# When a kernel asks for its values and its raw weights: two load rules of an attention, MLP and MoE kernel

## The chip, the cores and the metric

The kernel runs on one core of one Trainium2 chip. The metric is the device time of one execution in microseconds (us). Engines are named as in the profile: PE is TensorE (PEld its weight loads), DVE is VectorE, ACT is ScalarE, POOL is GpSimd, SP is the queue that starts the DMA transfers.

## The reference, cut

Three stages follow each other; 2304 tokens of width 512 run through all of them.

```python
# 1: attention, 4 batches x 8 heads x 576 positions x 64
q_d, k_d, v_d = means over 4 neighbouring positions
out_up = repeat(softmax(scale * q_d @ k_d.T) @ v_d, 4)
out_local = softmax(where(abs(i - j) < 4, scale * q @ k.T, -1e9)) @ v
x = out_up + out_local                      # 2304 x 512
# 2: MLP, w_in 512 x 2048, w_out 2048 x 512, both handed over as float64
x = softplus(x @ w_in) @ w_out
# 3: top-1 MoE over 8 experts (512 x 1024 x 512), gated by softmax of the router
```

## The kernel before

**Attention** is cut into jobs, listed in `jobs`. For each batch and pair of heads there is a `Down` job (the attention over means) and three `Local` jobs (one per 192 positions). A job has six stages (`st_T`, `st_S`, `st_E`, `st_N`, `st_Ta`, `st_PV`), and `attn_to` runs them software-pipelined, each stage some jobs behind the one before.

**Loads.** `loads` holds pairs (job number, function), sorted; after the first stage of job n, `load_after(n)` issues all loads whose number has come. A `Down` job's q, k and v (tiles `qr`, `kr`, `vr`, L136 and L139) are asked for four jobs ahead. A pair of `Local` jobs shares one value tile `lv` (L286, three DMAs of 70 KB with 256-byte rows); it is asked for right after the first `Local` job of the pair has been appended, with number `len(jobs) - 1`, that is, that job itself. The pool has three `lv` buffers.

**The MLP** works in six blocks of 384 tokens, each in 16 chunks: `mlp_H` (PE, tile `ph`, L571 in block 0, L574 later), a softplus on ACT and DVE (`gN`, L589 in block 0), `mlp_Y` (PE, tile `py`, L611 in block 0, L614 later). Block 0 multiplies in float32; later blocks split each weight chunk into two float32r parts: `split` copies on ACT (L474) and subtracts on POOL (L475) into tags `wis` and `wos`, two slots each.

**Float64 weights.** The 32 weight chunks (16 of w_in, 16 of w_out) arrive as int32 pairs and are turned into float32 by `from_f64`: one ACT operation (L435, |high word|) and four DVE operations (L436 to L439) per chunk of 128x512, into `wi` or `wo`. `conv` is the list of chunks; `conv_to` converts up to a count and calls `load_raw(i + 2)` before and after each. The raw tile of 512 KB (L452 for w_in, L456 for w_out) takes one of the six slots of the tag `raw`, which it shares with `vr`, with `qr` and `kr` of batches 1 to 3, and later with the outputs. `qr` and `kr` of batch 0 use the slots of `wis` and `wos`, which no split needs yet.

**What sets the order.** The program is recorded in the order of the loops; a scheduler then places instructions on each engine by priority and by when a slot is free. Each engine runs its own list strictly in order. SP too: a DMA that waits for a slot holds up all that are listed behind it. The last stretch before block 1 starts at about 180 us; block 0 with the conversion lies at about 64 to 180 us, the first attention jobs ahead of it. `warm` adds a small matmul (L265) behind attention matmuls in jobs 4 to 11.

Of the kernel before, what the change touches and what calls it, by code (L numbers as in the profile page):

```python
# [11 lines left out]
I32 = mybir.dt.int32  # L12
# [6 lines left out]
B, H, S, D = 4, 8, 576, 64  # L19
# [5 lines left out]
NPAIR = H // 2  # L25
# [5 lines left out]
NTH = S // TH  # L31
# [12 lines left out]
RAWB = 6  # L44
RAWB = 6
# [8 lines left out]
def band_attention__softplus_mlp__top1_moe(  # L54
# [44 lines left out]
    mlp = ctx.enter_context(tc.tile_pool(name="mlp", bufs=2))  # L99
# [4 lines left out]
    def ahead(n):  # L104

        return tc.high_priority(n) if n else nullcontext()
# [260 lines left out]
    jobs = []  # L367
    loads = []
    for b in range(B):
        if b in []:  # L370
            order = [(j, hp) for hp in range(NPAIR) for j in range(2)] + [(2, hp) for hp in range(NPAIR)]
        else:
            order = [(j, hp) for j in range(NTH) for hp in range(NPAIR)]
        for j, hp in order:
            if j == 0:
                jobs.append(Down(b, hp))
                loads.append((len(jobs) - 4, jobs[-1].load))
            jobs.append(Local(b, j, hp))
            if hp % 2 == 0:
                loads.append((len(jobs) - 1, jobs[-1].load_v))  # L380
    NJ = len(jobs)
    loads.sort(key=lambda x: x[0])

# [45 lines left out]
    def from_f64(raw, dst, on_g):  # L429

        lo, hi = raw[:, :, 0], raw[:, :, 1]
        t = mlp.tile([128, 512], I32, tag="cva", name="cva", bufs=2)
        A.activation(t.bitcast(F32), hi.bitcast(F32), AF.Abs)  # L435
        (G if on_g else V).tensor_scalar(t.bitcast(F32), t.bitcast(F32), F64_LEAST, None, ALU.max)  # L436
        V.tensor_scalar(t, t, 3, 0x3FFFFFF8, ALU.logical_shift_left, ALU.bitwise_and)
        V.scalar_tensor_tensor(t, hi, -0x40000000, t, ALU.bitwise_and, ALU.bitwise_or)
        V.scalar_tensor_tensor(dst.bitcast(I32), lo, 29, t, ALU.logical_shift_right, ALU.bitwise_or)  # L439
# [7 lines left out]
    def load_raw(n):  # L447
        while lpos[0] < min(n, len(conv)):
            kind, c = conv[lpos[0]]
            raw = mlp.tile([128, 512, 2], I32, tag="raw", name="raw", bufs=RAWB)  # L450
            if kind == "i":
                nc.sync.dma_start(  # L452
                    out=raw.rearrange("p (c f) w -> p c (f w)", c=CC),
                    in_=w_in[:, c * 128:(c + 1) * 128].bitcast(I32).rearrange("(c p) f -> p c f", p=128))
            else:
                nc.sync.dma_start(out=raw.rearrange("p f w -> p (f w)"),  # L456
                                  in_=w_out[c * 128:(c + 1) * 128, :].bitcast(I32))
            raws[lpos[0]] = raw
            lpos[0] += 1

    def conv_to(n):
        while cpos[0] < min(n, len(conv)):
            i = cpos[0]
            load_raw(i + 2)
            kind, c = conv[i]
            with ahead(0 if started[0] else -50):
                from_f64(raws.pop(i), wi[:, c].rearrange("p c f -> p (c f)") if kind == "i" else wo[:, c, :], i < 0)
            cpos[0] += 1
            load_raw(i + 2)

    def split(src, tag):
        w = mlp.tile([128, 2] + list(src.shape)[1:], F32R, tag=tag, name=tag, bufs=2)
# [5 lines left out]
    wis, wos = {}, {}  # L478
# [212 lines left out]
    for st in range(12 + LAG):  # L691
        attn_to(pre_end[st])
        if st >= C0 - 5 + LAG:
            conv_to((st - C0 + 5 - LAG) * CR // 4 + 1)
        if st == 9 + LAG:
            split_wi(0, 0)
# [15 lines left out]
    for i, (n, c) in enumerate(seq):  # L712
# [14 lines left out]
        if n == 0:  # L727
            conv_to(max(cpos[0], 3 + 2 * c + 1, CB + (33 - CB) * (2 * c + 1) // 26))
# [9 lines left out]
        if n == 0:  # L738
            conv_to(max(cpos[0], 3 + 2 * c + 2, CB + (33 - CB) * (2 * c + 2) // 26))
# [61 lines left out]
```

## Time and profile before

| | |
|---|---|
| three runs | 806.86, 814.97, 822.22 us; median 814.97 |
| profiled execution | 816.7 us, of which the span from first to last instruction is 814.8 |
| PE busy | 788.8 us (97% of the span), PEld 690.1 |
| DVE, ACT, POOL busy | 469.0, 452.8, 449.6 us (58, 56, 55%) |
| mean granted clock | 0.979 of full speed |
| HBM traffic | 45.05 MB read, 9.44 MB written, mean 67 GB/s |

PE's ends are modelled, so its busy share says where it did not wait, not that it ran at its peak. In the page's 40 slices (20 us each) PE's busy tenths begin 5899899 and stay at 9 afterwards; its granted clock reads 5 in the third slice. DVE's tenths are 6 to 9 in the first eight slices, and DMA's 9936677 in the first seven, after which both fall.

### The profile page before, as it was taken

The page shows a single profiled execution, that of the slowest core. Times are in us where ns is not written, and L with a number is a line of the kernel's source. Part 1 is how long each engine was busy: PE and PEld are TensorE (multiplying, and loading weights), DVE is VectorE, ACT ScalarE, POOL GpSimd, SP SyncE. Part 2 cuts the span into 40 slices and gives each one's busy share as a digit, 9 for nine tenths or more (in the row PEclk, how much of TensorE's full clock was granted, in tenths as well). Part 3 has the DMA queues.
Part 4 walks back from the last instruction along what each step waited for, and adds up shares of the span by engine and source line. Part 5 has one row for each costly group of instructions (what it writes and reads, how often), then busy time and mean ns, then how long its engine had stood idle before and what let it go on. Part 6 is the DMA issues. An engine that isn't in the chain of part 4 may idle for free.

```text
span 814.8 us, 14060 instructions
## 1 busy us (share of the span) xinstructions
PE 788.8 (97%) x5101; PEld 690.1 (85%) x5102; DVE 469.0 (58%) x1008; ACT 452.8 (56%) x1153; POOL 449.6 (55%) x435
## 2 busy tenths in 40 slices
PE   5899899999999999999999999999999999999996
PEld 4785556568899989989999999999998899898985
DVE  6958899736866667688655665648552422212111
ACT  5836676446556565766565656565654444444342
POOL 3534321315745566666656666666665666666662
PEclk9959999999989999999999999999999999999999
DMA  9936677302200321021000100063010201011011
GB/s 173 208 82 171 202 237 213 89 22 79 60 11 19 85 48 39 26 56 61 2 11 10 34 21 1 1 245 117 1 39 39 79 4 75 1 39 39 1 39 43
DMA packets 82167, 55.47 MB, mean 68 GB/s; under 512 B 61081, under 2 KB 73899, under 8 KB 82091
## 3 DMA queue, kind: packets, MB, share of 16 engines
q1 hardware_dynamic: 82091, 54.50, 23.9%
q8 instruction: 42, 0.69, 0.3%
q14 instruction: 34, 0.28, 0.1%
HBM read 45.05 MB, written 9.44 MB: 67 GB/s over the span
## 4 chain that ended last, share of the span: by engine, by line
PE 85%; DVE 6%; ACT 3%; DMA 2%; SPq 1%; issue 1%; POOL 0%; DVEq 0%; POOLq 0%; ACTq 0%
PE ph L574 32%; PE py L614 19%; PE py L658 12%; PE ph L571 4%; PE py L611 4%; PE pO L340 3%; PE pS L306 3%; PE pA L331 2%; PE pO L249 1%; PE pT L169 1%; PE pS L210 1%; PE pA L239 1%; DVE g L596 1%; SPq L136 1%; DMA qr<-in_q_dram 1%
## 5 line engine op out<-in xcount | busy, mean ns | idle before, releaser
L614 PE MATMUL py<-g,wos 128*128 128x384 f32 x960 | 192.4, 344 | 0.0
L574 PE MATMUL ph<-xT,wis 128*128 128x384 f32 x960 | 184.3, 339 | 0.3 <-ACT qkT L175 0.2
L614 PEld LDWEIGHTS py<-g,wos 128*128 128x128 f32 x960 | 166.9, 190 | 4.9 <-issue 1.7
L574 PEld LDWEIGHTS ph<-xT,wis 128*128 128x128 f32 x960 | 166.8, 188 | 2.5 <-issue 0.8
L475 POOL TENSOR_TENSOR wis<-wi,wis 128x512 fp32r<-128x512 f32 x80 | 107.0, 1338 | 60.6 <-ACT wis L474 55.0
L475 POOL TENSOR_TENSOR wos<-wo,wos 128x512 fp32r<-128x512 f32 x80 | 107.7, 1347 | 41.4 <-ACT wos L474 41.3
L574 PE MATMUL ph<-yT,wis 128*128 128x384 f32 x576 | 108.2, 336 | 0.0
L658 PE MATMUL py<-wos,g 128*128 128x512 f32 x432 | 106.6, 392 | 0.0
L574 PEld LDWEIGHTS ph<-yT,wis 128*128 128x128 f32 x576 | 101.5, 188 | 3.5
L601 DVE SCALAR_TENSOR_TENSOR g<-ph,g 128x384 fp32r<-128x384 f32 x48 | 26.7, 557 | 131.2 <-ACT g L600 131.2
L580 ACT ACTIVATE ga<-ph 128x384 f32<-128x384 f32 x96 | 46.8, 487 | 93.7 <-PE ph L574 76.3
L658 PEld LDWEIGHTS py<-wos,g 128*128 128x128 f32 x432 | 80.3, 188 | 15.3 <-ACT wis L474 0.6
L475 POOL TENSOR_TENSOR wos<-w2s,wos 128x512 fp32r<-128x512 f32 x48 | 64.0, 1334 | 48.7 <-ACT wos L474 48.7
L475 POOL TENSOR_TENSOR wis<-w1s,wis 128x512 fp32r<-128x512 f32 x48 | 61.8, 1288 | 30.5 <-ACT wis L474 30.4
L320 ACT ACTIVATE ls<-ls,lst 128x70 f32<-128x70 f32 x144 | 49.3, 344 | 42.0 <-DVE lst L314 38.1
L595 DVE SCALAR_TENSOR_TENSOR ga<-ph,ga 128x384 f32<-128x384 f32 x80 | 44.1, 551 | 49.6 <-ACT ga L582 49.1
L474 ACT CAST wos<-wo 128x512 fp32r<-128x512 f32 x80 | 49.5, 619 | 36.3 <-PE py L614 36.0
L597 DVE TENSOR_TENSOR g<-ga,g 128x384 fp32r<-128x384 f32 x80 | 65.7, 821 | 2.0
L326 POOL TENSOR_TENSOR ls<-ls,lst 128x210 f32<-128x210 f32 x48 | 29.1, 608 | 57.7 <-DVE lst L325 42.6
L600 ACT ACTIVATE g<-ph 128x384 fp32r<-128x384 f32 x48 | 23.6, 492 | 57.1 <-PE py L658 31.7
L596 DVE CAST g<-ga 128x384 fp32r<-128x384 f32 x80 | 49.9, 623 | 3.6 <-PE py L614 0.5
L582 ACT ACTIVATE ga<-ga 128x384 f32<-128x384 f32 x96 | 50.4, 525 | 1.9
(130 smaller groups left out, 1173.0 us busy)
## 6 DMA issues: line engine op xcount, KB each, us to landing
raw<-in_moe_w_in_dram SPq DMA_DIRECT2D x16, 512.0 KB
raw<-in_moe_w_out_dram SPq DMA_DIRECT2D x16, 512.0 KB
lv<-in_v_dram SPq DMA_DIRECT2D x72, 70.0 KB
qr<-in_q_dram SPq DMA_DIRECT2D x32, 144.0 KB
kr<-in_k_dram SPq DMA_DIRECT2D x32, 144.0 KB
vr<-in_v_dram SPq DMA_DIRECT2D x16, 288.0 KB
ydram<-y SPq DMA_DIRECT2D x12, 384.0 KB
yb<-ydram SPq DMA_DIRECT2D x6, 768.0 KB
```

Of the source, the lines that this page charges most:

```text
L320: A.activation(s[:, i, :], s[:, i, :], AF.Exp, bias=st[:, 0, i], accum_out=st[:, 1, i])
L474: A.copy(w[:, 0], src)
L475: G.tensor_tensor(out=w[:, 1], in0=src, in1=w[:, 0].bitcast(F32), op=ALU.subtract)
L571: T.matmul(ps[:, :TB], wi[:, c, cc, :], xT[n][:, cc, :], start=(cc == 0), stop=(cc == CC - 1))
L574: T.matmul(ps[:, :TB], wt[:, w, cc, :], xT[n][:, x, cc, :], start=(i == 0), stop=(i == 3 * CC - 1))
L580: A.activation(a, ps[:, :TB], AF.Abs)
L582: A.activation(a, a, AF.Ln, bias=1.0)
L595: V.scalar_tensor_tensor(a, ps[:, :TB], 0.0, a, ALU.max, ALU.add)
L596: (A.copy if n < 1 else V.tensor_copy)(g[:, 0, :], a)
L597: (G if n < 1 else V).tensor_tensor(out=g[:, 1, :], in0=a, in1=g[:, 0, :].bitcast(F32), op=ALU.subtract)
L614: T.matmul(yps[n][dc][:, :TB], w[:, a, dsl], g[:, b, :], start=(c == 0 and i == 0), stop=(c == NC1 - 1 and i == 2))
L658: T.matmul(yps[n][t], g[:, a, ts], w[:, b, :], start=(c == 0 and i == 0), stop=(c == NC2 - 1 and i == 2))
```

## The change

The first edit adds three to the job number at which a `Local` pair's value tile is asked for, with an upper limit near the end of the list. The second puts the raw float64 chunks of w_in into the two slots of `wis` and those of w_out into the two slots of `wos`, and leaves the `raw` slots to the attention tiles and outputs. The third asks for raw chunks three ahead of the conversion instead of two.

```diff
             if hp % 2 == 0:
-                loads.append((len(jobs) - 1, jobs[-1].load_v))
+                loads.append((min(len(jobs) + 2, B * NPAIR * (NTH + 1) - 1), jobs[-1].load_v))
 ...
-            raw = mlp.tile([128, 512, 2], I32, tag="raw", name="raw", bufs=RAWB)
+            raw = mlp.tile([128, 512, 2], I32, tag={"i": "wis", "o": "wos"}[kind], name="raw", bufs=2)
 ...
             i = cpos[0]
-            load_raw(i + 2)
+            load_raw(i + 3)
 ...
             cpos[0] += 1
-            load_raw(i + 2)
+            load_raw(i + 3)
```

SP's list of DMAs, from the second `Down` job's loads at the start of the program, before (x2 and x3 are so many DMAs):

```order
L136 DMA kr<-in_k_dram 96x6x64 x2
L139 DMA vr<-in_v_dram 72x4x256
L286 DMA lv<-in_v_dram 70x4x64 x3
L136 DMA qr<-in_q_dram 96x6x64 x2
L136 DMA kr<-in_k_dram 96x6x64 x2
L139 DMA vr<-in_v_dram 72x4x256
L136 DMA qr<-in_q_dram 96x6x64 x2
L136 DMA kr<-in_k_dram 96x6x64 x2
L139 DMA vr<-in_v_dram 72x4x256
L286 DMA lv<-in_v_dram 70x4x64 x3
L452 DMA raw<-in_moe_w_in_dram 128x4x256 x2
```

The same place of SP's list, of the change:

```order
L136 DMA kr<-in_k_dram 96x6x64 x2
L139 DMA vr<-in_v_dram 72x4x256
L136 DMA qr<-in_q_dram 96x6x64 x2
L136 DMA kr<-in_k_dram 96x6x64 x2
L139 DMA vr<-in_v_dram 72x4x256
L136 DMA qr<-in_q_dram 96x6x64 x2
L139 DMA vr<-in_v_dram 72x4x256
L136 DMA kr<-in_k_dram 96x6x64 x2
L286 DMA lv<-in_v_dram 70x4x64 x3
L452 DMA raw<-in_moe_w_in_dram 128x4x256
L456 DMA raw<-in_moe_w_out_dram 128x1024
```

The first value tile has moved from behind the second `Down` job to behind the fourth, and the first chunks follow it at once.

POOL's list at the end of batch 0's `Down` jobs (at about 34 to 52 us in the trace), before:

```order
L326 TENSOR_TENSOR ls<-ls,lst 128x210 x2
L475 TENSOR_TENSOR wis<-wi,wis 128x512
L150 TENSOR_TENSOR vr<-vr 72x4x128
L475 TENSOR_TENSOR wis<-wi,wis 128x512
L153 TENSOR_TENSOR vs<-vr 72x2x64 x2
L326 TENSOR_TENSOR ls<-ls,lst 128x210 x2
L475 TENSOR_TENSOR wos<-wo,wos 128x512
L150 TENSOR_TENSOR vr<-vr 72x4x128
```

The same place of POOL's list, of the change:

```order
L326 TENSOR_TENSOR ls<-ls,lst 128x210 x2
L150 TENSOR_TENSOR vr<-vr 72x4x128
L153 TENSOR_TENSOR vs<-vr 72x2x64 x2
L326 TENSOR_TENSOR ls<-ls,lst 128x210 x2
L150 TENSOR_TENSOR vr<-vr 72x4x128
```

The splits of block 1's first chunks (two of `wis` and one of `wos` here, a second `wos` some rows later) have left this place; in the change all four stand at the end of the conversion, ahead of the last part of block 0.

DVE's list around the first `gN` of block 0, the last eight rows up to it, before:

```order
L439 SCALAR_TENSOR_TENSOR wo<-raw,cva 128x512
L356 TENSOR_TENSOR xf<-pO,od 128x192
L231 RECIPROCAL dsm<-dsm 96x3
L334 COPY laT<-pA 70x384
L436 TENSOR_SCALAR cva<-cva 128x512
L364 CAST xT<-xf 128x192
L437 TENSOR_SCALAR cva<-cva 128x512
L589 SCALAR_TENSOR_TENSOR gN<-ph,ga 128x384
```

The same place of DVE's list, of the change:

```order
L231 RECIPROCAL dsm<-dsm 96x3
L356 TENSOR_TENSOR xf<-pO,od 128x192
L436 TENSOR_SCALAR cva<-cva 128x512
L364 CAST xT<-xf 128x192
L436 TENSOR_SCALAR cva<-cva 128x512
L437 TENSOR_SCALAR cva<-cva 128x512
L334 COPY laT<-pA 70x384
L437 TENSOR_SCALAR cva<-cva 128x512
L438 SCALAR_TENSOR_TENSOR cva<-raw,cva 128x512 x2
L589 SCALAR_TENSOR_TENSOR gN<-ph,ga 128x384
```

Counted from the start of DVE's list, five chunks are finished (L439) ahead of the first `gN` before, and seven in the change; of the next chunk two operations stand ahead of it before, and in the change three operations each of two further chunks.

## Rows read from the trace of the kernel before

**Rows 1.** Busy time by stretch: start:end, length, PE, PEld, DVE, ACT, POOL; PEclk, DMA share, GB/s

```profile
40.00:50.00 10.00, 10.00 (x68) 7.74 (x70) 7.69 (x17) 4.74 (x20) 6.21 (x7) 0.50 0.25 61
50.00:60.00 10.00, 10.00 (x84) 8.40 (x80) 3.97 (x15) 3.23 (x13) 2.43 (x5) 0.50 0.40 90
...
80.00:90.00 10.00, 7.51 (x43) 4.81 (x42) 5.34 (x12) 5.86 (x16) 3.17 (x5) 1.00 0.65 212
90.00:100.00 10.00, 10.00 (x61) 6.47 (x60) 9.97 (x23) 5.50 (x14) 3.97 (x5) 1.00 0.59 183
...
130.00:140.00 10.00, 10.00 (x53) 5.85 (x51) 9.96 (x25) 7.01 (x22) 1.59 (x2) 1.00 0.83 229
...
160.00:170.00 10.00, 10.00 (x59) 5.76 (x56) 3.86 (x13) 3.81 (x16) 3.25 (x6) 1.00 0.10 22
```

**Rows 2.** Timeline of PE: start, length, instruction, idle time before it and its releaser

```profile
15.85 1.19 PE L169 MATMUL pT<-ident,qr 96*128 96x96 f32 x6 [1.08 <-DMA qr<-in_q_dram]
...
25.60 0.73 PE L340 MATMUL pO<-laT,lv 70*64 70x64 f32 x12
...
39.34 0.66 PE L239 MATMUL pA<-ident,de 96*72 96x96 f32 x6 [1.41 <-DVE lst L324]
...
69.70 0.47 PE L169 MATMUL pT<-ident,kr 96*128 96x96 f32 x3 [0.90 <-DVE xf L356]
70.55 4.54 PE L571 MATMUL ph<-xN,wi 128*128 128x384 f32 x8 [0.39 <-ACT qkT L177]
...
79.14 2.74 PE L571 MATMUL ph<-xN,wi 128*128 128x384 f32 x8
...
89.30 2.85 PE L571 MATMUL ph<-xN,wi 128*128 128x384 f32 x8 [2.49 <-ACT de L225]
...
104.93 0.72 PE L249 MATMUL pO<-daT,vs 72*64 72x144 f32 x8 [1.42 <-ACT qkT L175]
```

**Rows 3.** Timeline of SP, the DMA queue's issues, in the first 20 us

```profile
8.47 1.37 SPq L286 DMA_DIRECT2D lv<-in_v_dram  x3
9.95 1.25 SPq L136 DMA_DIRECT2D qr<-in_q_dram  x2
...
18.70 1.37 SPq L286 DMA_DIRECT2D lv<-in_v_dram  x3
```

**Rows 4.** The chain that ended last, in order of time: start, length, what

```profile
10.56 5.15 DMA qr<-in_q_dram
...
64.40 4.42 DMA raw<-in_moe_w_in_dram
...
77.02 3.47 DMA lv<-in_v_dram
...
82.71 3.63 DMA raw<-in_moe_w_out_dram
```

**Rows 5.** Timeline of DVE and POOL, at 18 us and at 36 to 39 us

```profile
17.82 0.59 DVE L232 TENSOR_TENSOR de<-de,dsm 96x432 f32<-96x432 f32 x1
...
36.05 1.26 POOL L475 TENSOR_TENSOR wis<-wi,wis 128x512 fp32r<-128x512 f32 x1
36.19 1.42 DVE L437 TENSOR_SCALAR cva<-cva 128x512 int32<-128x512 int32 x1
...
37.29 1.44 POOL L150 TENSOR_TENSOR vr<-vr 72x512 f32<-72x512 f32 x1
...
37.53 1.66 DVE L232 TENSOR_TENSOR de<-de,dsm 96x432 f32<-96x432 f32 x1
```

**Rows 6.** Timeline of DVE, one chunk's operations and its longest wait for one

```profile
75.11 0.41 DVE L436 TENSOR_SCALAR cva<-cva 128x512 f32<-128x512 f32 x1
...
76.05 0.41 DVE L437 TENSOR_SCALAR cva<-cva 128x512 int32<-128x512 int32 x1
...
76.67 0.68 DVE L438 SCALAR_TENSOR_TENSOR cva<-raw,cva 128x512 int32<-128x512 int32 x1
...
78.27 0.68 DVE L439 SCALAR_TENSOR_TENSOR wo<-raw,cva 128x512 int32<-128x512 int32 x1
...
83.68 0.43 DVE L436 TENSOR_SCALAR cva<-cva 128x512 f32<-128x512 f32 x1 [3.81 <-ACT cva L435]
```

## Prediction

> **What bounds the kernel now.** I read the page's busy shares first: PE is at 97%, so little can be gained anywhere but where PE waits or runs at half clock. The busy time by stretch then tells where that is. From 110 us to 180 us every 10 us stretch reads 10.00 for PE at a granted clock of 1.00; one of these seven stands in [rows 1]. From the end of block 0's first quarter, then, PE is the bound and nothing in front of it shortens its own work. Ahead of that PE waits, and the timeline of PE names the waits [rows 2]: 1.08 us for a q tile, 1.41 us behind DVE at 39 us, 0.90 and 0.39 us at 70 us, 2.49 us at 87 to 89 us, 1.42 us at 103 to 105 us. And it has two slow stretches: 40 to 60 us at clock 0.50 with PE busy 10.00 of 10 [rows 1], which is the lower of its two levels (1.2 instead of 2.4 GHz), and the eight matmuls at 70.55 that took 4.54 us where the same eight take 2.74 us at 79 us [rows 2]. The listed orders differ only up to the last raw chunk's load; behind it, at about 160 us, SP's list is the same in both. So the change acts in the first 165 us, and what it can give is an earlier start of the unbroken PE work at 105 us.
>
> **The value tiles, asked for three jobs later.** Nothing is removed: each tile still has three DMAs. The first `lv` leaves SP's list from in front of the third `Down` job's q. SP spent 1.37 us on it (8.47 us) and reached that q only at 9.95 us [rows 3]; q then took 5.15 us [rows 4], and PE waited 1.08 us for it at 15.85 us [rows 2]. SP now reaches q 1.4 us earlier. PE cannot take all of it, since its own attention work ends just before: I take the wait itself, 1.0 us. Bounds: 0 if ACT or DVE hold PE there, 2.5 if the lighter queue also shortens the landing by as much as the wait again. The other side is that `lv` itself is late. It was used first at 25.60 us [rows 2]; SP was through the four `Down` jobs at 18.70 us [rows 3], so without 1.37 us of `lv` in front it gets there at 17.3 us, issues it in 1.4 us, and by the slowest landing in these rows, 5.15 us, it is there at 23.9 us. PE wants it at 25.60 less 1.0, at 24.6 us. That cover is thin, 0.7 us; I cost it at nothing, and up to 2 us if the landing is half as long again.
>
> **The splits that leave 36 to 44 us.** With `wis` and `wos` taken by raw chunks, block 1's first splits can no longer run here. One of them held POOL for 1.26 us from 36.05, and DVE's L437 beside it took 1.42 us where 0.41 is usual [rows 5, 6]. L232 right behind took 1.66 us instead of 0.59 us, but beside POOL's L150 (37.29, 1.44 us), which stays [rows 5]. So of the delay ahead of PE's 1.41 us wait about 1.0 us (1.42 less 0.41) belongs to the split: 1.0 us, with bounds 0 (L150 slides into its place and blocks as long) and 1.41 (the whole wait). The four splits now stand at about 150 to 165 us, where POOL is busy 3.25 us of 10 and DVE 3.86 [rows 1]: 4 x 1.26 = 5.0 us of POOL, and if each delayed DVE by 1.0 us, 4.0 us of DVE, fit into 6.7 and 6.1 idle us. Cost nothing; without that cover 4.0 us.
>
> The Trainium skill (SBUF — State Buffer, Who interferes with whom) says that VectorE and GpSimd share a port pair which whoever starts first holds for a whole instruction, while the other is blocked. By that rule the splits cost DVE time wherever they stand, here and later, and moving them gives only what the new place has idle; the sum above would be the same, as the later place has room.
>
> **Raw chunks in their own slots, three ahead.** The chain of waits from 64 to 89 us goes through transfers: a raw w_in tile 4.42 us, an `lv` 3.47 us, a raw w_out tile 3.63 us [rows 4]. The last waited for a slot of `raw` that a `vr` still held, and SP was stuck behind it. DVE stood still for 3.81 us for a chunk [rows 6], PE 2.49 us at 87 us, and behind these late chunks DVE was full (9.97 of 10, [rows 1]) and PE waited another 1.42 us at 103 us [rows 2]. With separate slots the conversion runs ahead: in DVE's list seven chunks stand ahead of the first `gN` instead of five. One chunk costs 0.41 + 0.41 + 0.68 + 0.68 = 2.2 us [rows 6], so two are 4.4 us, and that is more than the 1.42 us. I take both waits: 2.49 + 1.42 = 3.9 us.
>
> The 0.90 + 0.39 = 1.3 us at 70 us I don't take. Ahead of the first `gN` there now stand two chunks more, and three operations each of two further ones (3.0 us) instead of two of one (0.8 us): 4.4 + 3.0 - 0.8 = 6.6 us more DVE work in front of the first `py` matmul. DVE has room for it at 40 to 60 us: 20 - 7.69 - 3.97 = 8.3 us idle [rows 1]. But some of that work stands right in front of `gN`, behind the idle place, and so this wait goes on as one for `gN`. Bounds of the part: 0, and 3.9 + 1.3 = 5.2 us.
>
> **The half clock.** From 39 us on, after a wait of 1.41 us, PE did its work at half rate for 20 us, with no wait in between [rows 1, 2]. At full clock PE would need 10 us of the 20; then DVE is next, with 7.69 + 3.97 = 11.7 us there, and 18.3 us if all of the 6.6 us move in. So the stretch would shrink by 1.7 to 8.3 us. The wait ahead of it shrinks by my sum to 0.4 us, yet waits of 2.49 and 1.42 us at 87 and 103 us brought no drop (clock 1.00 at 80 to 100 us, [rows 1]), so length alone does not decide, and I leave the clock as it is: 0, to 8.3 us of gain. The 1.8 us at 70.55 (4.54 less 2.74) I leave too. The Trainium skill (TensorE: Matmul & The Clock Gate, What's actually happening) has the array throttled by default and released by activity. By it 20 us of busy PE would have ended the low clock early and this part would be near nothing; the rows show 10.00 of 10 busy at 0.50 all the while, so the full 20 us are at stake.
>
> **Sum.** 1.0 + 1.0 + 3.9 = 5.9 us. The profiled execution took 816.7 us, which gives 810.8 us. It lies 1.7 us above the median of the three runs, 814.97, and inside their spread of 806.86 to 822.22; I forecast 810.
>
> **Rivals.**
> - *The clock stays up too* (22 in 100). For it: the wait ahead of the drop loses the part that a split caused. Against it: small matmuls go on in the same order. About 5 us more, the middle of 1.7 and 8.3: 805.8. With every bound at its best, 2.5 + 1.4 + 5.2 + 1.8 + 8.3 = 19.2 us, it would be 797.5.
> - *The loads were hidden, and DVE is the bound* (20 in 100). DVE at 9.97 of 10 in 90 to 100 us and at 9.96 in 130 to 140 us [rows 1] speaks for it: earlier raw tiles then only wait for DVE, the 6.6 us in front of the first `gN` take back what the start gave, and the change does not do what it says. 816.7. Against it: the 3.81 us wait of DVE for a chunk.
> - *SP's list blocks the chunks* (8 in 100), slower. Freed of raw chunks, the `raw` slots let the later `Down` jobs' q, k and v be listed up to two jobs further ahead, and each waits in SP's list for a transpose on PE or a `vs` on POOL, with raw chunks behind it. Four such places lie in block 0; if each cost PE the 2.49 us that a late chunk cost before, it is 10.0 us, and the 3.9 us are not gained: 816.7 - 2.0 + 10.0 = 824.7. It decides once the waits add up to more than the 5.9 us. Against it: up to eleven chunks are listed ahead of the first of these waits, more than PE needs by then.
>
> **How the numbers follow.** The forecast has 50 in 100. A measurement of this kernel can tell about 2% from no change, that is 798.7 and 831.3 around 814.97. Below 798.7 only the clock rival near its best bound arrives, with the runs' spread about 10 in 100. Above 831.3 lies the slower rival only with that spread: 4 in 100. The range of 799 to 821 takes in the forecast, the hidden loads, and the clock rival down to near its bound, and leaves out most of the slower rival.
>
> **What would show it.** Right: q of the third `Down` job without a wait on PE near 15 us; no L475 before 140 us, and L437 near 0.41 us at 36 us; no DVE wait of 3 us for a raw chunk at 80 us, and PE without the waits of 2.49 and 1.42 us; a start of the first L574 about 6 us ahead of the 180 us of before. Wrong: PE waiting for `lv` at the first L340, for `gN` at the first L611 by much more than 1.3 us, or DVE waiting for chunks at which SP stood behind a q or k. A clock of 1.00 at 40 to 60 us would put the time near the first rival.

## The result and the profile after

The changed kernel is a little slower, by some 1%. Its median is 823.55 us (818.47 to 825.81, 20 runs) against 816.9 us (806.86 to 823.16, 20 runs) of the kernel before, measured beside it; the ratio is 1.0117, with a 95% interval of 1.0094 to 1.0141. (A ratio leaves out the executions that lie more than 1.5% above the fastest of their kernel, and so isn't the quotient of the medians.) The forecast was 810. The profiled execution has a span of 820.0 us (814.8 before) at a mean granted clock of 0.981 (0.979 before), so the two profiles can be laid side by side.

From the page of the changed kernel, the busy line of the engines and the share of the chain that ended last:

```profile
PE 787.6 (96%) x5101; PEld 686.4 (84%) x5102; DVE 469.9 (57%) x1008; ACT 454.2 (55%) x1153; POOL 459.7 (56%) x435
...
PE 78%; DVE 13%; issue 3%; DMA 2%; SPq 1%; ACT 1%; DVEq 0%; ACTq 0%
```

PE is still the engine that is full, but VectorE (DVE in the views) now stands for 13% of the chain, 6% before. Most of the growth is between 60 and 150 us: VectorE's pieces of the chain there add up to 65.9 us, 13.0 us before.

All of the difference lies ahead of block 1's first chunk. The first L574 starts at 179.96 us before and at 185.35 us after, 5.4 us later; from there to the end it is 634.8 and 634.7 us. So one view, with three stretches up to that point, sums it up (start:end, length, then PE, PEld, DVE, ACT, POOL; PEclk, DMA share, GB/s). Length less PE's busy time is what PE waited. The kernel before:

```profile
10.00:60.00 50.00, 46.31 (x393) 37.98 (x393) 38.80 (x89) 31.50 (x118) 20.91 (x28) 0.80 0.76 154
60.00:110.00 50.00, 44.76 (x279) 29.11 (x278) 44.40 (x99) 33.82 (x103) 17.57 (x25) 0.96 0.67 198
110.00:179.96 69.96, 69.96 (x401) 42.18 (x399) 53.97 (x129) 37.01 (x107) 18.34 (x23) 1.00 0.47 133
```

The changed kernel:

```profile
10.00:60.00 50.00, 44.89 (x420) 36.54 (x420) 37.95 (x92) 31.84 (x118) 16.43 (x24) 0.83 0.88 190
60.00:110.00 50.00, 41.75 (x240) 26.54 (x239) 47.91 (x106) 32.62 (x97) 25.76 (x27) 0.93 0.79 214
110.00:185.35 75.35, 74.01 (x414) 43.62 (x412) 52.03 (x120) 38.41 (x113) 24.34 (x24) 1.00 0.31 90
```

PE waited 3.69 + 5.24 + 0.00 = 8.9 us before and 5.11 + 8.25 + 1.34 = 14.7 us after: 5.8 us more. By an estimate from the granted clock of the two stretches, the clock costs the same in both: 50 x (0.20 + 0.04) = 12.0 us before, 50 x (0.17 + 0.07) = 12.0 us after. Between these two executions, then, the loss is waiting. The timeline of PE in the changed kernel names the waits (start, length, instruction, idle time before it and its releaser); they answer [rows 2]:

```profile
14.59 0.69 PE L169 MATMUL pT<-ident,qr 96*128 96x96 f32 x6 [0.21 <-DMA qr<-in_q_dram]
16.73 1.47 PE L210 MATMUL pS<-dkT,dbd 128*96 128x144 f32 x6 [1.45 <-DVE dkT L188]
...
28.48 0.46 PE L249 MATMUL pO<-daT,vs 72*64 72x144 f32 x2 [1.57 <-ACT daT L242]
...
40.47 0.76 PE L239 MATMUL pA<-ident,de 96*72 96x96 f32 x6 [1.73 <-DVE lst L325]
...
69.75 0.47 PE L169 MATMUL pT<-ident,kr 96*128 96x96 f32 x3 [1.93 <-ACT de L225]
...
73.41 5.33 PE L571 MATMUL ph<-xN,wi 128*128 128x384 f32 x8 [2.28 <-DVE laT L334]
...
107.04 0.72 PE L249 MATMUL pO<-daT,vs 72*64 72x144 f32 x8 [2.21 <-ACT qkT L175]
```

The q wait shrank from 1.08 to 0.21 us and the 2.49 us at 89 us is gone, as forecast. In their place stand 1.45 us at 16.73, 1.57 at 28.48 (0.66 before), 1.73 at 40.47 (1.41 before), 1.93 and 2.28 us at 70 to 73, and 2.21 at 107 (1.42 before). The stretches of the changed kernel, as [rows 1] and some beside them:

```profile
30.00:40.00 10.00, 8.75 (x95) 6.92 (x93) 9.50 (x24) 6.64 (x28) 3.33 (x5) 1.00 1.07 220
40.00:50.00 10.00, 9.53 (x66) 7.41 (x66) 3.19 (x12) 4.64 (x18) 3.47 (x6) 0.54 0.82 198
50.00:60.00 10.00, 10.00 (x116) 8.32 (x114) 7.36 (x22) 4.55 (x16) 2.58 (x4) 0.77 0.36 79
60.00:70.00 10.00, 7.05 (x56) 4.75 (x54) 9.23 (x27) 8.21 (x34) 7.22 (x8) 1.00 1.01 240
70.00:80.00 10.00, 7.27 (x40) 4.04 (x39) 8.81 (x18) 5.03 (x11) 8.42 (x9) 0.66 0.73 206
...
140.00:150.00 10.00, 9.65 (x58) 5.74 (x58) 9.93 (x18) 5.29 (x15) 6.25 (x5) 1.00 0.19 53
150.00:160.00 10.00, 9.24 (x44) 4.88 (x44) 4.30 (x9) 4.98 (x16) 2.69 (x4) 1.00 0.00 0
```

VectorE is busy only 3.19 us at 40 to 50 (7.69 before, [rows 1]) and 7.36 at 50 to 60 (3.97 before). At 30 to 40 us, where PE comes to wait for it, it is as full as it was (9.50, 9.88 before). From 80 us to 150 us it is nearly full; before, it had room once there, at 80 to 90 us (5.34), where the changed kernel reads 9.93.

Did the chunks come earlier? Yes. VectorE's groups by line at 60 to 110 us (count, busy and mean, idle before and its releaser), first before, then after:

```profile
L438 DVE SCALAR_TENSOR_TENSOR cva<-raw,cva 128x512 int32<-128x512 int32 x12 | 8.5, 705 | 0.1
L436 DVE TENSOR_SCALAR cva<-cva 128x512 f32<-128x512 f32 x12 | 5.3, 445 | 3.9 <-ACT cva L435 3.8
```

```profile
L438 DVE SCALAR_TENSOR_TENSOR cva<-raw,cva 128x512 int32<-128x512 int32 x14 | 11.3, 812 | 0.1
L436 DVE TENSOR_SCALAR cva<-cva 128x512 f32<-128x512 f32 x15 | 7.8, 521 | 0.8 <-ACT cva L435 0.8
```

VectorE's wait for chunks fell from 3.9 to 0.8 us, and its last conversion operation (L439) starts at 149.9 us instead of 154.8. That gain is real, and nothing waited for it: in the kernel before PE had no wait behind 110 us.

### The profile page after: what moved, and what is told of

Read it like the earlier page. It is cut to its first block, busy times and chain, and to the rows that moved or that the text cites. A ratio compares the mean times of both kernels' runs of the same rounds, so it can differ in the third digit from the quotient of the medians.

```text
span 820.0 us, 14051 instructions
## 1 busy us (share of the span) xinstructions
PE 787.6 (96%) x5101; PEld 686.4 (84%) x5102; DVE 469.9 (57%) x1008; ACT 454.2 (55%) x1153; POOL 459.7 (56%) x435
## 4 chain that ended last, share of the span: by engine, by line
PE 78%; DVE 13%; issue 3%; DMA 2%; SPq 1%; ACT 1%; DVEq 0%; ACTq 0%
PE ph L574 32%; PE py L614 19%; PE py L658 12%; PE pO L340 2%; DVE cva L438 2%; PE ph L571 2%; PE pS L306 2%; PE py L611 2%; PE pA L331 2%; DVE cva L436 1%; SPq L136 1%; PE pO L249 1%; DVE cva L437 1%; DVE wi L439 1%; PE pT L169 1%
## 5 line engine op out<-in xcount | busy, mean ns | idle before, releaser
L574 PE MATMUL ph<-xT,wis 128*128 128x384 f32 x960 | 184.0, 339 | 0.3 <-ACT qkT L175 0.2
L574 PEld LDWEIGHTS ph<-xT,wis 128*128 128x128 f32 x960 | 166.5, 188 | 2.5 <-issue 0.8
L475 POOL TENSOR_TENSOR wis<-wi,wis 128x512 fp32r<-128x512 f32 x80 | 107.0, 1338 | 64.7 <-ACT wis L474 58.5
L475 POOL TENSOR_TENSOR wos<-wo,wos 128x512 fp32r<-128x512 f32 x80 | 107.8, 1348 | 42.6 <-ACT wos L474 42.5
L574 PE MATMUL ph<-yT,wis 128*128 128x384 f32 x576 | 108.2, 336 | 0.0
L574 PEld LDWEIGHTS ph<-yT,wis 128*128 128x128 f32 x576 | 101.5, 188 | 3.5
L475 POOL TENSOR_TENSOR wos<-w2s,wos 128x512 fp32r<-128x512 f32 x48 | 64.0, 1334 | 48.5 <-ACT wos L474 48.5
L475 POOL TENSOR_TENSOR wis<-w1s,wis 128x512 fp32r<-128x512 f32 x48 | 62.4, 1299 | 30.2 <-ACT wis L474 30.0
L326 POOL TENSOR_TENSOR ls<-ls,lst 128x210 f32<-128x210 f32 x48 | 31.5, 656 | 71.9 <-DVE lst L325 43.6
```

What stands on the lines that cost most here:

```text
L326: G.tensor_tensor(out=s, in0=s, in1=st[:, 1].to_broadcast([128, 3, KW]), op=ALU.mult)
L475: G.tensor_tensor(out=w[:, 1], in0=src, in1=w[:, 0].bitcast(F32), op=ALU.subtract)
L574: T.matmul(ps[:, :TB], wt[:, w, cc, :], xT[n][:, x, cc, :], start=(i == 0), stop=(i == 3 * CC - 1))
```

## The experiments

The expectations name the theories by letters. A: the own slots are the loss, through conversions ahead of PE's work and splits that move to 140 to 152 us. B: late value tiles make the waits in the first 40 us and let the clock fall. C: SP's list blocks. D and L came after the first four runs: D, a stop of PE at 40 us, made by conversions that come early, lets the clock fall; L, POOL's splits at 140 to 152 us block VectorE.

The kernel before ran beside each of the four groups of experiments, 108 times in all, from 805.91 to 824.03 us. How fast it was goes with the clock granted in the execution: 38 of the 108 had a mean clock of 0.989 or more (a line drawn by eye: the clocks go over without a gap) and a median of 809.0 us, the other 70 had 817.4 us. The 20 executions of the changed kernel all lie under that line, with a median 6.1 us over that of those 70: at a like clock the loss is about that of the two profiles, 5.8 us. The table counts for each kernel the executions at or over that line. "Waits" is PE's waiting from 10 us to the first L574, from the three stretches as above, in one execution of each kernel; where PE runs at half clock it waits less for the others, so two such numbers compare best at a like clock. The execution profiled of e4 is its fastest, the only one of seven over the line (816.4 us), and that of e5 its fastest too.

| kernel | median us (lowest to highest, runs) | ratio, 95% | clock 0.989 and over | waits us | first L571, L574 |
|---|---|---|---|---|---|
| before | 815.4 (805.9 to 824.0, 108) | | 38 of 108 | 8.9 | 64.5, 180.0 |
| changed | 823.6 (818.5 to 825.8, 20) | 1.0117, 1.0094 to 1.0141 | 0 of 20 | 14.7 | 63.9, 185.4 |
| e1 value tiles | 811.0 (808.2 to 821.6, 12) | 0.9975, 0.9939 to 1.0010 | 9 of 12 | 9.0 | 57.7, 173.8 |
| e2 slots | 810.4 (808.7 to 813.5, 12) | 0.9980, 0.9951 to 1.0009 | 12 of 12 | 11.6 | 55.1, 173.8 |
| e3 ahead | 810.8 (805.7 to 820.8, 12) | 0.9954, 0.9912 to 0.9997 | 7 of 12 | 10.9 | 59.9, 175.2 |
| e4 tiles, slots | 824.1 (816.4 to 827.0, 7) | 1.0135, 1.0095 to 1.0175 | 1 of 7 | 12.4 | 62.2, 181.2 |
| e10 tiles, ahead | 816.5 (809.7 to 819.1, 10) | 0.9991, 0.9945 to 1.0037 | 3 of 10 | 11.0 | 63.9, 181.6 |
| e11 slots, ahead | 813.5 (810.1 to 816.9, 10) | 1.0005, 0.9961 to 1.0050 | 8 of 10 | 11.5 | 54.8, 175.4 |
| e5 changed, filled | 816.9 (814.0 to 821.7, 10) | 1.0036, 0.9993 to 1.0078 | 4 of 10 | 12.1 | 61.6, 180.3 |
| e6 before, filled | 809.6 (807.2 to 815.2, 10) | 0.9992, 0.9950 to 1.0033 | 10 of 10 | 8.3 | 59.0, 176.6 |
| e8 changed, no split on POOL | 821.6 (819.2 to 826.6, 4) | 1.0133, 1.0053 to 1.0212 | 0 of 4 | 12.7 | 64.5, 184.9 |
| e9 changed, held | 814.2 (809.4 to 820.5, 10) | 1.0008, 0.9954 to 1.0063 | 6 of 10 | 11.3 | 57.2, 179.2 |
| e13 before, held | 813.5 (809.5 to 824.4, 10) | 0.9967, 0.9927 to 1.0008 | 3 of 10 | 11.1 | 61.7, 177.7 |
| e14 slots, held | 809.1 (807.4 to 815.6, 10) | 0.9962, 0.9920 to 1.0004 | 10 of 10 | 11.0 | 56.0, 173.6 |
| e12 tiles, ahead, filled | 809.0 (807.3 to 812.2, 10) | 0.9958, 0.9914 to 1.0001 | 10 of 10 | 10.0 | 60.9, 175.1 |
| e7 ahead, filled | 808.2 (806.3 to 814.0, 10) | 0.9943, 0.9902 to 0.9985 | 10 of 10 | 9.0 | 58.2, 172.5 |
| e15 ahead, filled, again | 808.1 (806.0 to 810.5, 6) | 0.9888, 0.9838 to 0.9939 | 6 of 6 | 9.6 | 58.0, 173.6 |

### One part alone (e1, e2, e3)

The value tiles alone:

```diff
-                loads.append((len(jobs) - 1, jobs[-1].load_v))
+                loads.append((min(len(jobs) + 2, B * NPAIR * (NTH + 1) - 1), jobs[-1].load_v))
```

> Only the value tiles are asked for three jobs later; raw chunks stay in the raw slots, two ahead. Theory A (the slots are the loss: conversions run ahead of the work that PE waits for, and the first splits of block 1 move to 140 to 152 us, where DVE is still full): no loss, 812 to 818 us, and L475 at 34 to 44 us as before. Theory B (the loss is the early attention: waits there decide whether the clock falls at 40 us, and the late value tiles made them): 820 us or more, with half clock at 40 to 60 us in the profile. Rival C of the prediction (SP's list): no loss.

The slots alone:

```diff
-            raw = mlp.tile([128, 512, 2], I32, tag="raw", name="raw", bufs=RAWB)
+            raw = mlp.tile([128, 512, 2], I32, tag={"i": "wis", "o": "wos"}[kind], name="raw", bufs=2)
```

> Only the raw chunks move into the slots of wis and wos; still two ahead, value tiles as before. Theory A: most of the loss, 819 to 824 us; the four L475 at 140 us or later with DVE full beside them, and the first L574 3 to 5 us later than before. Theory B: no loss, 812 to 818 us. Rival C: part of the loss, with DVE waiting for chunks while SP stands behind a q, k or v.

Three ahead alone (twice, ahead of the conversion and behind it):

```diff
-            load_raw(i + 2)
+            load_raw(i + 3)
```

> Only the distance of the raw requests goes from two to three. Theory A: within 0.5% of before, 811 to 820 us, as slots and splits stay. Theory B: the same. Rival C: a loss only if SP's list is longer blocked, up to 820 us.

None of the three is slow: 811.0, 810.4 and 810.8 us. So no part is the loss by itself, and A fails in its plain form: with the slots alone VectorE is just as full and the splits come as late, and the time is 1.4 us over that of the better executions of before (809.0). The slots alone kept the clock at 1.00 in all three stretches of their profile (timeline of PE at 36 us, the transposes that wait at 39 to 40 us in the other kernels):

```profile
36.02 0.49 PE L265 MATMUL pO<-ident 128*128 128x128 f32 x2
36.34 0.66 PE L239 MATMUL pA<-ident,de 96*72 96x96 f32 x6
```

There they come 3 to 4 us earlier than in the kernels before and after and don't wait at all, since VectorE scaled their rows (L232) at 33.11 us. Counted by L439, one chunk is finished ahead of that L232. In the kernel before it is two (at 32.80 and 34.68 us, L232 at 37.53), in the changed kernel three (30.27, 35.33 and 37.21 us, L232 at 39.55). With the value tiles alone it is three as well (L232 at 40.21): it is the value tiles that put one more chunk there.

The value tiles alone show what their part does without the rest. Timeline of VectorE in e1, and below it that of PE:

```profile
15.82 0.74 DVE L188 TENSOR_REDUCE dkT<-qkT 128x144 f32<-128x576 f32 x1
```

```profile
14.73 1.14 PE L169 MATMUL pT<-ident,qr 96*128 96x96 f32 x6
16.70 0.95 PE L210 MATMUL pS<-dkT,dbd 128*96 128x144 f32 x6 [0.83 <-DVE dkT L188]
```

The q tile is there, and PE now waits for `dkT` instead, which VectorE starts at 15.82 us; in the kernel before it started at 15.99 us. PE's product (L210) starts at 16.70 us where it started at 16.87 us before: of the 1.08 us, 0.17 us is gained. ScalarE takes more than that back. Its timeline in the changed kernel (e1 has the same order), at 27 us:

```profile
27.48 0.66 ACT L435 ACTIVATE cva<-raw 128x512 f32<-128x512 f32 x1
28.05 0.38 ACT L242 COPY daT<-pA 72x288 f32<-72x288 f32 x1
```

The conversion of a raw chunk (L435) now stands in front of the copy of `daT` (L242), which came at 27.21 us before, with the conversion behind it at 28.66 us. PE waits 1.57 us for that copy instead of 0.66 (1.74 in e1, 1.34 in e4, 0.65 to 0.67 in e2 and e3, which lack the moved value tiles).

### Two parts (e4, e10, e11)

Value tiles and slots, that is the change with `load_raw(i + 2)` kept:

```diff
-            load_raw(i + 3)
+            load_raw(i + 2)
```

> The change without its third edit: value tiles three jobs later and raw chunks in the slots of wis and wos, but two ahead. PE's, DVE's and ACT's lists are then the same as in the change; only SP's and POOL's differ. Theories A and B: as slow as the change, 821 to 825 us, since those lists carry the loss. Rival C: back to 815 to 819 us, since SP's list is another.

Value tiles and three ahead, that is the change with the old slots:

```diff
-            raw = mlp.tile([128, 512, 2], I32, tag={"i": "wis", "o": "wos"}[kind], name="raw", bufs=2)
+            raw = mlp.tile([128, 512, 2], I32, tag="raw", name="raw", bufs=RAWB)
```

> Value tiles three jobs later, and weight tiles asked for three ahead in the slots they had before (no own slots). If the loss belongs to the slots, which keep VectorE full to 150 us and put the split at 140 to 152 us: 808 to 812, as each of the two alone. If it belongs to value tiles that come late beside any chunk that comes early: 818 to 824, as with value tiles and slots.

Slots and three ahead, that is the change with the value tiles as before:

```diff
-                loads.append((min(len(jobs) + 2, B * NPAIR * (NTH + 1) - 1), jobs[-1].load_v))
+                loads.append((len(jobs) - 1, jobs[-1].load_v))
```

> Own slots and three ahead, value tiles as before. If the slots lose by themselves as soon as the chunks come early: 816 to 823. If it takes the late value tiles too (TensorE's wait of 1.57 us at 28 us and the stop at 40 us, that the kernel with the slots alone does not have): 808 to 812, clock at 1.00 from 40 to 60 us.

The loss is there with value tiles and slots (824.1) and needs no third part. Without the moved value tiles it goes (813.5, and no wait at 40 us in the profile). Value tiles and three ahead are between: 816.5 us, no loss against the kernel before (ratio 0.9991), and in neither of the two ranges expected, as the 813.5 isn't either. In the profile of that kernel PE stops even longer at 40 us, and the clock read 0.53 at 40 to 50 us (timeline of PE in e10):

```profile
41.91 1.15 PE L239 MATMUL pA<-ident,de 96*72 96x96 f32 x6 [3.18 <-DVE lst L324]
```

So what loses is the value tiles that leave the head of SP's list together with the slots; that value tiles lose with any chunk that comes early isn't shown. B holds so far as it names the place. C fails: with two ahead SP's list is another and the loss is the same (824.1), and in the changed kernel SP stood behind PE or POOL for a q, k or v for at most 1.9 us at a time, with the chunks early all the same.

### The stop at 40 us filled in part (e5, e6)

Four more warm-up multiplications behind one attention product, at the end of which PE stops. In the changed kernel and in the kernel before:

```diff
-            for i in range(1):
+            for i in range(5 if nwarm.append(0) or len(nwarm) in (8,) else 1):
                 T.matmul(ps[:, 384:384 + 128], ident, ident[:, :128], start=True, stop=True)
```

> The changed kernel, with four more warm-up multiplications (128x128 each, two records of about 0.2 us) put behind the score product of the first attention, where TensorE stood 1.73 us at 40.47 us before its transposes (waiting for the softmax of one local job) and then ran at a granted clock of 0.50 until 54 us. Nothing else is reordered on TensorE there. Theory D (the clock): the stop at 40 us is what lets the clock fall; with the stop filled it stays at 1.00 from 38 to 60 us, the first expert chunk (L571) starts at 57 to 58 us instead of 63.9, and the time falls from 823.5 to 816 to 819. Theory L (POOL's lock at 140 to 152 us): the stretch from the first chunk to the first chunk of block 1 is the bound whatever the start is, so half of what the start gains is eaten and the time stays at 821 to 824. If the clock falls anyway, the time stays at 823 and D is not tested.

> The kernel before, with the same four multiplications at the same place (its stop is 1.41 us at 39.34 us, its clock 0.50 from 42 to 58 us). Its times in 49 runs went from 806.9 to 824, the lower ones with a mean granted clock of 0.99, the higher ones with 0.98 and less. Theory D: the clock stays at 1.00 there, the runs come together at 807 to 810, median about 808.5, and the first chunk starts at 56 to 58 us instead of 64.5. If the spread of before has another cause, the median stays at 814 to 816 and the spread of 15 us stays.

823.6 became 816.9, and 815.4 became 809.6. The stretch behind the stop, in the changed kernel with the fill:

```profile
40.00:50.00 10.00, 9.16 (x107) 7.42 (x106) 6.17 (x19) 6.03 (x25) 5.28 (x9) 1.00 1.02 226
50.00:60.00 10.00, 8.17 (x101) 6.76 (x101) 10.00 (x28) 7.61 (x27) 4.68 (x5) 0.83 0.83 193
```

0.54 has become 1.00 at 40 to 50 us. The kernel before, with the fill, had a clock of 0.99 or more in all ten executions, against 38 of 108 at 0.989 or more without it. So what PE does at 40 us bears on the clock behind it in both kernels, and the fill gives 6.6 and 5.8 us on the medians. The stop itself didn't go: PE still waits 0.84 us behind the multiplications in the changed kernel (1.73 without them) and 1.18 us in the kernel before (1.41). In the changed kernel the clock still fell later (0.83 at 50 to 60 us), only four of ten executions reached 0.989, and the first L571 starts at 61.6 us where D had 57 to 58. The two kernels also show what the clock at 40 us doesn't explain: 7.3 us between them are left with the fill in both.

### The splits taken off POOL (e8)

ScalarE copies the value where POOL subtracted, for the four splits at 140 to 152 us; this kernel leaves out the low halves of these four weight chunks.

```diff
-            G.tensor_tensor(out=w[:, 1], in0=src, in1=w[:, 0].bitcast(F32), op=ALU.subtract)
+            (A.copy(w[:, 1], src) if nspl.append(0) or len(nspl) in (1, 2, 4, 6) else G.tensor_tensor(out=w[:, 1], in0=src, in1=w[:, 0].bitcast(F32), op=ALU.subtract))
```

> The changed kernel, in which the low halves of the four split weight tiles that POOL worked out at 140 to 152 us (1.44, 2.58, 1.51 and 1.27 us) are copied by ScalarE instead of being subtracted by POOL; the low half of these four tiles is thus wrong, everything else is computed, and TensorE's order is the same. Theory L: beside POOL's four subtractions VectorE's instructions took 1.37, 1.24, 1.64 and 1.18 us instead of 0.41, 0.16, 0.68 and 0.26, 3.9 us more in a stretch in which VectorE is full (9.93 of 10) and TensorE waits for it; they go, block 1's first chunk starts 3 to 4 us earlier, and the time falls from 823.5 to 819 to 820.5. Theory D alone (only the clock at 40 us): the stretch has room, the time stays at 822.5 to 824.

The rows that it is about, from the timelines of POOL and, below, of VectorE in the changed kernel:

```profile
140.10 1.44 POOL L475 TENSOR_TENSOR wis<-wi,wis 128x512 fp32r<-128x512 f32 x1
145.29 2.58 POOL L475 TENSOR_TENSOR wis<-wi,wis 128x512 fp32r<-128x512 f32 x1 [3.75 <-ACT wis L474]
```

```profile
140.45 1.37 DVE L437 TENSOR_SCALAR cva<-cva 128x512 int32<-128x512 int32 x1
...
146.65 1.24 DVE L324 TENSOR_SCALAR lst<-lst 128x3 f32<-128x3 f32 x1
...
148.25 1.64 DVE L438 SCALAR_TENSOR_TENSOR cva<-raw,cva 128x512 int32<-128x512 int32 x1
```

The waits behind 110 us went from 1.34 to 0.07 us:

```profile
110.00:184.90 74.90, 74.83 (x416) 44.73 (x414) 49.02 (x120) 40.42 (x120) 17.41 (x20) 0.98 0.31 90
```

But the first L574 came only 0.5 us earlier, at 184.85 us; in this execution the clock was down once, from 109 to 112 us. The median is 821.6, from four runs of 819.2 to 826.6: a gain of at most 2 us, not clear of the spread, where L said 3 to 4. The delays of VectorE are there; PE felt 1.3 us of them.

### The first conversions held back (e9, e13, e14)

```diff
-            with ahead(0 if started[0] else -50):
+            with ahead(0 if started[0] else -100):
```

in the changed kernel, in the kernel before, and in the kernel with the slots alone.

> The changed kernel, with the conversions of the first chunks given a lower rank in the order (100 places back instead of 50). On TensorE nothing is reordered ahead of 55 us; on VectorE the scaling of the softmax rows (L232, which the transposes at 40.47 us wait for) comes ahead of two of the conversion instructions (0.68 and 1.01 us) that it stood behind, and of 1.5 us of softmax work of a later job. Theory D (stop and clock): TensorE's stop of 1.73 us at 40 us shrinks under 0.8 us, the clock holds at 0.8 to 1.00 from 40 to 60 us, first expert chunk at 57 to 60 us, time 815 to 818, as when the stop was filled (816.9). If early conversions are not what makes that stop, it stays at 1.4 us or more, with the clock at 0.5 behind it and 822 to 824.

> The kernel before, with the conversions of the first chunks given the lower rank (100 places back) that took the changed kernel from 823.5 to 814.2. Its own stop at 39.34 us (1.41 us) came with POOL's split at 36.05 us (1.26 us), beside which conversions took 1.42 and 1.66 us. Theory D (the stop decides, whatever makes it): the scaling of the softmax rows comes ahead of one conversion less, the stop shrinks to about 1 us, the clock falls in fewer runs, 809 to 814. If the lower rank helps only where the chunks come early: 814 to 818, as before, and the gain in the changed kernel is a repair of what the change did.

> Own slots alone (810.4), with the lower rank for the first conversions. It has no stop at 40 us to repair. Theory D: 808.5 to 812, no change. If the lower rank is a gain by itself (VectorE free for attention), 805 to 808.

The edit gives all conversions ahead of block 0 a lower rank. The changed kernel goes from 823.6 to 814.2, with the same instructions, and the same order on PE up to 55 us. What moved is the conversions, on ScalarE and VectorE. VectorE's timeline in the changed kernel:

```profile
35.33 0.68 DVE L439 SCALAR_TENSOR_TENSOR wi<-raw,cva 128x512 int32<-128x512 int32 x1
35.92 0.68 DVE L438 SCALAR_TENSOR_TENSOR cva<-raw,cva 128x512 int32<-128x512 int32 x1
...
37.21 1.01 DVE L439 SCALAR_TENSOR_TENSOR wo<-raw,cva 128x512 int32<-128x512 int32 x1
38.14 0.16 DVE L231 RECIPROCAL dsm<-dsm 96x3 f32<-96x3 f32 x1
38.22 1.14 DVE L324 TENSOR_SCALAR lst<-lst 128x3 f32<-128x3 f32 x1
39.28 0.36 DVE L314 TENSOR_REDUCE lst<-ls 128x3 f32<-128x210 f32 x1
39.55 0.77 DVE L232 TENSOR_TENSOR de<-de,dsm 96x432 f32<-96x432 f32 x1
```

The scaling that PE waits for (L232) comes at 39.55 us, behind three finished chunks where it was two before. Counted in the timelines, four instructions more stand ahead of it than before: one L438, one L439, one L314 and one L324, at their usual lengths 0.68 + 0.68 + 0.36 + 0.16 = 1.9 us. The two slow instructions, 1.01 and 1.14 us, ran beside a `TENSOR_TENSOR` of POOL (L150, 1.71 us from 37.62). With the conversions held back, VectorE and then PE:

```profile
38.65 0.86 DVE L232 TENSOR_TENSOR de<-de,dsm 96x432 f32<-96x432 f32 x1
```

```profile
39.65 0.66 PE L239 MATMUL pA<-ident,de 96*72 96x96 f32 x6 [0.50 <-DVE de L232]
```

The scaling comes 0.9 us earlier, PE's stop is 0.50 instead of 1.73 us, and the clock reads 1.00 from 40 to 50 us. Over the three stretches:

```profile
10.00:60.00 50.00, 46.49 (x446) 37.57 (x447) 41.40 (x106) 37.54 (x141) 20.46 (x30) 0.97 1.01 218
60.00:110.00 50.00, 44.02 (x248) 27.44 (x247) 47.25 (x99) 31.60 (x82) 22.48 (x24) 0.96 0.77 209
110.00:179.23 69.23, 67.41 (x378) 39.73 (x377) 46.04 (x110) 35.03 (x103) 23.85 (x23) 1.00 0.27 81
```

PE waits 11.3 us instead of 14.7, and the clock costs 50 x (0.03 + 0.04) = 3.5 us instead of 12. The kernel before gains 2 us by the same edit (813.5), with its stop as it was (1.47 us at 39.35); the slots alone stay at 809.1, within 1.3 us of 810.4. So holding back is for the most part a repair of what the change did, and the early rank of the first conversions is shown as a cause of the loss, enough to bring the median level with the kernel before (ratio 1.0008). Part of the 9.4 us is the clock, which stayed at 0.989 and over in six executions of ten instead of none of 20; the four under that line have a median of 820.2, 3.4 us better than the changed kernel.

That the place at 34 to 40 us is what counts is argued, not shown. The edit moved conversions elsewhere too: ScalarE's copy of `daT` is back in front of the conversion, and PE waits 0.70 us for it at 28 us instead of 1.57. And the value tiles alone have the same three chunks ahead of L232, but nine of twelve executions with the clock up; why, no run shows.

It isn't the whole of it. Of the changed kernel with held conversions, the six executions with a clock of 0.989 and more have a median of 812.7 us, 3.7 us over the 809.0 of before. Its waits stand behind 60 us: 5.98 + 1.82 = 7.8 us, against 5.24 us before. This belongs to the slots: from 60 us to the first L574, PE waits 6.1 to 9.6 us in the profiles of all eight kernels that have them, and 3.4 to 5.7 us in the nine that don't. POOL's groups at 60 to 110 us, and VectorE's L437, before and after:

```profile
L150 POOL TENSOR_TENSOR vr<-vr 72x512 f32<-72x512 f32 x2 | 2.5, 1266 | 6.1 <-DMA lv<-in_v_dram 6.1
L185 POOL TENSOR_TENSOR ds<-qkT 128x288 f32<-128x288 f32 x3 | 2.2, 749 | 8.3 <-ACT qkT L177 8.3
L437 DVE TENSOR_SCALAR cva<-cva 128x512 int32<-128x512 int32 x12 | 9.3, 771 | 0.1
```

```profile
L150 POOL TENSOR_TENSOR vr<-vr 72x512 f32<-72x512 f32 x3 | 4.8, 1615 | 6.8 <-DVE wo L439 6.8
L185 POOL TENSOR_TENSOR ds<-qkT 128x288 f32<-128x288 f32 x3 | 4.0, 1328 | 3.3 <-PE pA L239 2.3 <-ACT qkT L177 1.0
L437 DVE TENSOR_SCALAR cva<-cva 128x512 int32<-128x512 int32 x14 | 6.8, 486 | 0.0
```

With the `raw` slots free of chunks, later `Down` jobs' v tiles are loaded and summed earlier: the ninth and tenth loads of a `vr` come at 86 and 110 us instead of 146 and 155. POOL's instructions get longer beside VectorE (L185 749 to 1328 ns). VectorE's don't on the whole: L438 goes from 705 to 812 ns but L437 from 771 to 486, and the four operations of a chunk take 2.6 us in both; what it has more of in this stretch is chunks (L438 14 times instead of 12). That POOL's earlier work and the earlier chunks make the last 3.7 us is argued from these rows and not shown by a run of its own.

### A version that beats both (e12, e7, e15)

The multiplications of e5, with value tiles and three ahead in the old slots, and with three ahead alone:

> Value tiles three jobs later, three ahead, slots as before, and the four multiplications in the stop at 40 us. Theory D: no half clock ahead of 60 us, 806 to 810. With late value tiles as the loss by themselves (1 us more of waits at 28 us, nothing gained at 15 us): 809 to 812, over the 808.2 of three ahead with the multiplications.

> Only the third part of the change (weight tiles asked for three ahead, in the slots they had before), with the same four multiplications. Alone, the part gave 810.8 with runs from 805.7 to 820.8. Theory D: the clock stays up in all runs and the time is 805.5 to 808, under the kernel before by 0.8 to 1.2%. If the stop at 40 us is not what decides the clock, 809 to 812 with the spread as it was.

> Three ahead in the old slots, with the four multiplications in the stop at 40 us, the fastest so far (808.2, ratio 0.994 with 0.990 to 0.9985), measured closer. Theory D: 806 to 809, in nearly all runs with a mean clock of 0.99 and more, ratio 0.990 to 0.995. If the first measurement was luck of the clock: 809 to 812, with runs over 815 among them.

Three ahead in the old slots with the stop filled is the best: 808.2 and 808.1 us, ratios 0.9943 (0.9902 to 0.9985) and 0.9888 (0.9838 to 0.9939), with a clock of 0.99 or more in all 16 executions. Adding the moved value tiles gives 809.0, no gain. Most of it is the fill, which by itself gives the kernel before 809.6; the 1.4 us between that and three ahead with the fill lie inside the overlap of their runs.

## Why the prediction was wrong, point by point

The step that failed is the largest term of the sum: the two waits at 87 to 105 us, which late chunks had made, were booked as a gain of 3.9 us. The chunks did come early, and from 60 to 110 us PE waited 3.0 us more instead, for attention's work on ScalarE and VectorE. The other terms failed in the same way, by less.

- **Value tiles, 1.0 us.** The q tile came as forecast. What failed is that the wait itself was taken as the gain: VectorE was behind it. Its `dkT` starts at 15.99 us before and 15.86 after, and PE's L210 at 16.87 and 16.73, so 0.14 us was gained. The prediction had this as its lower bound (0 if VectorE holds PE) and chose the other end, though VectorE's timeline at 13 to 16 us would have shown it. And 0.91 us went at 28 us (1.57 against 0.66), because a conversion got in front of `daT` on ScalarE. `lv` itself, the danger that was priced, was not late. The two places come to about -0.8 us.
- **Splits that leave 36 to 44 us, 1.0 us.** The split did leave, and L437 took 0.42 us there, as said. But the place did not stay empty: the last operations of a third chunk moved up in front of L232, and L150 ran beside L439 and L324 (1.01 and 1.14 us). PE's stop grew from 1.41 to 1.73 us instead of falling to 0.4. The bound (0, L150 slides in) thought of POOL only. The sum priced seven chunks instead of five ahead of the first `gN`, but never asked what on VectorE they pass on the way.
- **The room on VectorE at 40 to 60 us.** The 6.6 us of work ahead of the first `gN` were to go into 8.3 idle us there. They did not: VectorE was busy 3.19 + 7.36 = 10.6 us there, 1.1 us less than before, and the place that filled up is 80 to 90 us (9.93 against 5.34). The place of a conversion is set by the list, not by where VectorE is idle in the run.
- **Chunks in own slots, 3.9 us.** VectorE's wait for chunks went (3.9 to 0.8 us), and so did PE's 2.49 us. But the waits at 60 to 110 us grew from 5.24 to 8.25 us: 1.93 and 2.28 us at 70 to 73, 2.21 at 107, all released by attention's work on ScalarE and VectorE. Ahead of the one at 73 us (L334) VectorE's list has three conversion operations from 70.5 us on; ahead of the one at 107 us a conversion of ScalarE stood in the kernel before, too. That chunks in own slots come earlier was right; that PE would start earlier for it was not: -3.0 instead of +3.9 us. All eight kernels with the slots wait more behind 60 us than any of the nine without.
- **Splits at nothing.** They came at 140 to 152 us and not at 150 to 165, on a VectorE at 9.93 of 10. The waits behind 110 us are 1.34 us, and with POOL's part taken away 0.07: -1.3 us, inside the bound of 4.0 that was named for the cover gone.
- **The half clock left as it is.** True between the two profiles (12.0 us in each). But the sum was made against a profile with the clock down, and the forecast took its gain off that without asking how often it was down: in 70 of 108 executions before the mean clock was under 0.989, in all 20 after.
- **The rivals.** SP's list gave 824.7 us, near the time measured, for another reason: no chunk was late. That it came near is luck. Its premise, that free `raw` slots pull later `Down` loads forward, did come true, and shows on POOL. The hidden loads, with VectorE as the bound, come nearest in kind: the chunks that come earlier keep VectorE full earlier, and nothing waited for the last of them.

Of the sum: forecast +5.9 us; measured -5.8 us of waits, of which 1.4 us lie before 60 us, 3.0 us at 60 to 110 and 1.3 us behind. That the 6.6 us between the medians are near it is in part the clock, which was up in some executions of before and in none of after.

## What to carry to other kernels

Work that is made ready earlier need not go into the idle place that one has in mind. Here it moved up in the list of an engine that keeps its order, and the price was what it passed there; so list what then stands behind it and who waits for that. When a load stops being what ends a wait, look at the second-latest input of the waiting instruction before booking the wait as a gain. And where a stop of TensorE is followed by a long stretch at half clock, look at that stop first: filling it in part was worth 5.8 us in the kernel before, more than any of the three parts alone.

## What the runs showed of the hardware

A stop of PE of 1.4 to 1.7 us at 40 us was followed by a granted clock of 0.50, the lower of the two levels, for about 14 us in the changed kernel and 20 us before (from the granted clock of the stretches), with PE waiting for nothing in that time. With four more multiplications ahead of the stop, whose results nobody reads, or with the stop cut to 0.50 us, the same place read 1.00. The length alone does not decide: with value tiles, three ahead and the fill, a stop of 1.38 us at 43.61 left the clock at 1.00 for the next 10 us. And in the profiles of e3 (stop 1.41 us) and e4 (1.72 us) the 10 us behind it read 0.83, which is the lower level for about 3.4 us only. What ends it earlier there no run shows.

VectorE and POOL lengthen each other: L324, 0.16 us by itself, took 1.14 us beside POOL's L150 and 1.24 us beside L475; and L475, 1.27 us at 151.62, took 2.58 us at 145.29, where VectorE was full. The Trainium skill (SBUF — State Buffer, Who interferes with whom) says that the two share a port pair which one of them holds for a whole instruction; these rows agree.
